# Twenty-eight steps of row preparation ahead of expert 0's last products, where three were

## The chip, the cores and the metric

The kernel runs on one core of a Trainium2 chip. The metric is the device time of one execution in microseconds (us); three runs of the kernel before gave a median of 1004.69 us (1001.67 to 1005.63). One further execution was recorded by the hardware profiler and is the source of every row below.

The core's engines each have a queue that is worked off in order: TensorE (PE in the rows; its weight loads are PEld), VectorE (DVE), ScalarE (ACT), GpSimd (POOL) and SyncE (SP). An instruction whose inputs or buffer are not ready holds up all that stands behind it on its engine.

## The reference

An attention over 32 memory slots gives `x` (4608 rows of 512), and a mixture of 8 experts with the two best per row follows. The change lies in the expert part, of which this is the core:

```python
top2 = np.argpartition(-noisy_logits, 2, axis=1)[:, :2]     # two experts per row
for e in range(E):                                           # 8 experts
    for k in range(2):
        mask = top2[:, k] == e
        h = np.maximum(x[mask] @ w1[e], 0.0)                 # 512 -> 1024
        out[mask] += top2_w[mask, k, None] * (h @ w2[e])     # 1024 -> 512
```

## The kernel before

Attention and routing come first. They write the attention's rows to a table in DRAM (`xs`) and, for each expert, a list of row numbers and weights (`lst`). Each expert then takes up to 1216 rows from its list. All products are made in float16 from a high and a low half of each factor, so that every float32 tile has to be split: ACT copies it to float16 (the high half), and DVE subtracts that copy from it (the low half).

Expert 0 is worked in four groups of rows, called (0,0) to (0,3). The first three are mixed into the attention; the fourth has 448 rows. Every later expert has two groups, of 320 and 288 rows: (1,0), (1,1), (2,0) and so on. For expert 0, `mm1` (line 924) makes the first layer in eight chunks `f` of 12 matmuls (line 935) into one of three PSUM banks `mp`; ACT reads each chunk out (`r`, line 941, two buffers), DVE makes its halves `hh` and `hl` (lines 942 and 943). `mm2` (line 945) makes the second layer (line 965), ACT scales the result by the row weights (`y`, line 977), and POOL adds it to the output with an indirect DMA (line 995).

The later experts use a scheme of seven products for the first layer (`mm1_sums`, line 837; its matmuls are line 851), which takes sums and differences of quarters of the rows and of the weights. The preparation of the rows is `gather_sums` (line 781), a generator that is run in steps. For each of three blocks of a group (128, 128 and 64 pairs of rows for (1,0)) it

- fetches two tiles of rows, `gsum` and `gtile`, by indirect DMAs that POOL issues (line 793);
- makes sums and differences on DVE (lines 810, 811, 825, 826);
- splits three tiles into halves (ACT line 820, DVE line 821), two of 512 columns called `ghalf` and one of 768 called `gsplit`, and has SyncE issue a transposing DMA of each into `xt`, which the matmuls read (line 822). `ghalf` has two buffers in the pool that `gather` uses too, and a third one of its own; a buffer is free again when its transpose has landed.

Between blocks it yields "wait" until a count of ticks has passed (`FAR` and `MOVE`, 8 each). Expert 0's own rows are prepared by `gather` (line 740: fetch in line 757, split in lines 768 and 771, transpose in line 772). The weights of expert 1 are prepared by `w_prep_sums` (line 635): four sums of squares on ACT (line 644), a short chain on DVE that turns them into a scale (lines 647 and 374 to 381, ending in `wsc`), and then splits of the weights and of their sums (ACT line 654, DVE line 657; sums in lines 668 to 672).

The order of the work is made in two stages. The program text calls generators step by step, and each call gets a priority in the order of the calls; a planner then lays out each engine's queue from those priorities and from a model of the time. In the part around the change, `all_rows` (line 1169) chains the row preparation of all groups into one generator `allr`, beginning with (0,3) and then (1,0). `run(it, n)` (line 1003) takes n steps of a generator, and a "wait" that it gets counts as a step and advances the tick by one. `side` holds the generators from which `step_side` (line 1016) takes one step at a time between the products. `pace` (line 775) ties an instruction to a matmul that was issued a little earlier, if there is one on its list; the list is filled only in `step_side`. Ahead of the loop over groups, in order: the weight load of expert 1, the steps of `allr`, and four steps of the weight preparation `pq[1]` (the four sums of squares). The loop begins with (0,3); `need` (line 1176) runs `allr` until the rows of the group at hand are prepared.

Of the kernel before, what the change touches and what calls it, by code (L numbers as in the profile page):

```python
# [61 lines left out]
def tile_attn_moe(ctx, tc, q_t, phi_t, kv, wgn, noise, w1, w2, out):  # L62
# [536 lines left out]
    def w_load(e, i):  # L599
        WS[e, i] = {}  # L600
        loaded[e, i] = ticks[0]
        for c in (3, 0, 1, 2) if e == 1 and i == 0 else (0, 2, 1, 3) if e else range(4):
            s = WS[e, i][c] = mpool.tile([128, 1024], F32, name="stg%d" % c)
            d = nc.sync.dma_start(s, (w1, w2)[i][e, c])
            if e == 0:
                after(d, "kv", BUF["w2" if i else "w1"] + c * BUF["ws"])
# [396 lines left out]
    def run(it, n=10 ** 9):  # L1003
        for _ in range(n):
            x = next(it, "end")
            if x == "end":
                return
            ticks[0] += x == "wait"
# [160 lines left out]
    def all_rows():  # L1169
        for k, x in enumerate(seq):  # L1170
            yield from rows_in(k, *x)
            ready.add(x)
    allr = all_rows()
# [3 lines left out]
            run(it, 1)  # L1177
    pq[1] = prep(1)
    w_load(1, 0)
    run(allr, 3)  # L1180
    run(pq[1], 4)
    side += [allr, pq[1]]
    for k, (e, g) in enumerate(seq):
# [78 lines left out]
```

## Time and profile before

| quantity | value |
|---|---|
| median of three runs | 1004.69 us (1001.67 to 1005.63) |
| profiled execution | 1002.9 us, of which the span from first to last instruction is 1000.9 us |
| TensorE busy | 918.5 us, 92% of the span |
| DVE, ACT, POOL busy | 616.2, 579.4, 337.2 us |
| mean granted TensorE clock | 0.974 of full speed |
| chain that ended last | TensorE 66%, DMA 10%, DVE 9%, ACT 4% |

How to read it: "busy" counts an engine's instructions, not its waits. The chain that ended last follows the program back from its last instruction, at each step to what released that step. The granted clock is 1.00 at 2.4 GHz and 0.50 at 1.2 GHz. In a timeline a bracket gives the idle time of the engine just before an instruction and what released it; a time from one row to another on a different engine is a difference of start times.

### The profile page before, as it was taken

How to read it: one execution, taken by the hardware profiler on the slowest of the kernel's cores; microseconds unless marked ns; L12 is line 12 of the kernel's file. 1: busy time of each engine (PE TensorE's matmuls, PEld its weight loads, DVE VectorE, ACT ScalarE, POOL GpSimd, SP SyncE). 2: the span in 40 equal slices, each digit the busy share in tenths (PEclk: the TensorE clock that was granted, in tenths of full speed). 3: DMA queues.
4: the chain of work that ended last, by engine and by line, in shares of the span. 5: the costliest groups of instructions: out<-in, count | busy, mean ns of one | idle time of the engine just before them, and what ended most of it. 6: DMA issues, size and time to landing. Idle time of an engine off the chain costs nothing.

```text
span 1000.9 us, 17556 instructions
## 1 busy us (share of the span) xinstructions
PE 918.5 (92%) x6440; PEld 540.0 (54%) x6440; DVE 616.2 (62%) x1407; ACT 579.4 (58%) x1187; POOL 337.2 (34%) x307
## 2 busy tenths in 40 slices
PE   3898996989894999999999999999999999999995
PEld 2465654655342555465555656564646564656552
DVE  1547788642662858575866776576849585957140
ACT  3577775532542756656665767576757666765241
POOL 3122654774222142414141514232333323240303
PEclk9999997999997999999999999999999999999997
DMA  9999979937687778776786869586947794775403
GB/s 319 316 308 324 352 268 344 224 83 119 121 140 98 161 120 162 149 146 99 180 151 116 132 147 179 98 163 120 204 85 148 141 213 74 158 123 82 63 1 48
DMA packets 197910, 162.01 MB, mean 162 GB/s; under 512 B 152064, under 2 KB 162496, under 8 KB 195776
## 3 DMA queue, kind: packets, MB, share of 16 engines
q1 hardware_dynamic: 178144, 120.43, 49.2%
q0 software_dynamic: 19680, 40.45, 23.9%
q8 instruction: 51, 0.84, 0.4%
q14 instruction: 35, 0.29, 0.1%
HBM read 86.77 MB, written 41.07 MB: 128 GB/s over the span
## 4 chain that ended last, share of the span: by engine, by line
PE 66%; DMA 10%; DVE 9%; ACT 4%; issue 4%; POOL 2%; SPq 2%; POOLq 0%; ACTq 0%; DVEq 0%
PE ps L965 18%; PE mp L965 15%; PE ps L851 13%; PE mp L851 7%; DMA xt<-ghalf 4%; PE pb L851 3%; PE mp L935 3%; SPq L703 2%; DMA stg<-in_w 1%; PE xp L470 1%; PE xp L355 1%; DMA phs<-in_phi_t 1%; PE tr L435 1%; PE tr L315 1%; DVE wl L657 1%
## 5 line engine op out<-in xcount | busy, mean ns | idle before, releaser
L995 POOL DMA_INDIRECT out<-y,lt x80 | 137.3, 1716 | 269.3 <-ACT y L977 239.1
L965 PEld LDWEIGHTS <-hh 128*128 128x128 f16 (+2 forms) x1504 | 122.3, 99 | 145.2 <-issue 15.9
L851 PE MATMUL ps<-xt,wh 128*128 128x320 f16 (+1 forms) x560 | 140.1, 295 | 17.6 <-DMA xt<-ghalf 15.1
L965 PE MATMUL ps<-wh,hl 128*128 128x512 f16 (+2 forms) x400 | 125.4, 380 | 0.0
L965 PE MATMUL ps<-wl,hh 128*128 128x512 f16 (+2 forms) x400 | 124.9, 380 | 0.0
L965 PE MATMUL ps<-wh,hh 128*128 128x512 f16 (+2 forms) x400 | 121.5, 380 | 0.0
L851 PEld LDWEIGHTS <-wh 128*128 128x128 f16 x896 | 87.0, 98 | 54.7 <-DMA xt<-ghalf 16.1
L965 PE MATMUL mp<-wh,hh 128*128 128x512 f16 (+2 forms) x352 | 113.0, 380 | 3.5 <-ACT hh L864 1.3
L965 PE MATMUL mp<-wl,hh 128*128 128x512 f16 (+2 forms) x352 | 113.0, 380 | 0.0
L965 PE MATMUL mp<-wh,hl 128*128 128x512 f16 (+2 forms) x352 | 112.0, 380 | 0.8 <-DVE hl L865 0.8
L965 PEld LDWEIGHTS <-hl 128*128 128x128 f16 (+2 forms) x752 | 63.1, 99 | 72.5 <-issue 6.9
L851 PE MATMUL ps<-xt,whx 128*128 128x320 f16 (+1 forms) x336 | 96.3, 292 | 0.0
L793 POOL DMA_INDIRECT gtile<-xs,lt x28 | 32.2, 1151 | 186.8 <-DVE ghalf L821 148.6
L654 ACT ACTIVATE wh<-stg,wsc 128x512 f16<-128x512 f32 x112 | 76.1, 713 | 30.8 <-DVE wsc L381 19.6
L570 POOL DMA_INDIRECT lst<-gent,gidx x72 | 72.1, 1002 | 37.0 <-issue 20.0
L657 DVE SCALAR_TENSOR_TENSOR wl<-stg,wsc,wh 128x1024 f16<-128x1024 f32 (+1 forms) x63 | 73.0, 1161 | 14.9 <-ACT wh L654 14.5
L851 PEld LDWEIGHTS <-whx 128*128 128x128 f16 x672 | 65.8, 98 | 28.0 <-issue 3.8
L644 ACT ACTIVATE wl<-stg 128x1024 bf16<-128x1024 f32 x56 | 58.6, 1047 | 28.9 <-DMA stg<-in_w 22.2
L851 PE MATMUL ps<-xt,wl 128*128 128x320 f16 (+1 forms) x280 | 73.7, 295 | 0.0
L857 ACT ACTIVATE r<-ps 128x320 f32<-128x320 f32 (+1 forms) x112 | 46.8, 421 | 39.7 <-PE ps L851 26.4
L793 POOL DMA_INDIRECT gsum<-xs,lt x42 | 48.1, 1144 | 63.1 <-DVE gsplit L821 52.8
L851 PE MATMUL mp<-xt,wh 128*128 128x320 f16 (+1 forms) x224 | 64.8, 292 | 0.9 <-DMA xt<-ghalf 0.7
(214 smaller groups left out, 1852.8 us busy)
## 6 DMA issues: line engine op xcount, KB each, us to landing
stg<-in_w SPq DMA_DIRECT2D x64, 512.0 KB
kvs<-in_kv SPq DMA_DIRECT2D x16, 1024.0 KB
out<-zt SPq DMA_DIRECT2D x38, 256.0 KB
qs<-in_q_t SPq DMA_DIRECT2D x16, 576.0 KB
xs<-xr SPq DMA_DIRECT2D x36, 256.0 KB
phs<-in_phi_t SPq DMA_DIRECT2D x16, 288.0 KB
kvs<-in_kv SPq DMA_DIRECT2D x16, 128.0 KB
xt<-ghalf SPq DMA_TRANSPOSE x88
```

The costliest lines, as they stand in the source:

```text
L315: mark["kv", u] = T.matmul(pk[h * 32:(h + 1) * 32, 0, :], es[:K, c, h * 32:(h + 1) * 32], kvs[:K, c, h, :], start=(c == 0), stop=(c == 4))
L570: sc = G.indirect_dma_start(out=lst[:, :], out_offset=bass.IndirectOffsetOnAxis(ap=idx[:, j, k:k + 1], axis=0), in_=ent[:, j, k, :], in_of ...
L644: (id if first else pace)(A.activation(wl[:, c * 1024:c * 1024 + 1024].bitcast(BF16), s[c], AF.Square, accum_out=am[:, c:c + 1]))
L654: (id if first else pace)(A.activation(h[:, o + k:o + k + 512], x[:, k:k + 512], AF.Identity, scale=sc))
L657: V.scalar_tensor_tensor(l[:, o:o + n], x, sc, h[:, o:o + n], op0=OP.mult, op1=OP.subtract)
L703: d = nc.sync.dma_start(dst, src)
L793: G.indirect_dma_start(out=x[:n], out_offset=None, in_=xs[:, :], in_offset=bass.IndirectOffsetOnAxis(ap=ix.bitcast(I32), axis=0))
L851: mark["pe"] = T.matmul(ps[:, :nh], t[w][:, o:o + 128], xt[:, 4 * k0 + 2 * n0 * lo + 2 * (a - k0) + c, :nh], start=(first and m == 0), sto ...
L857: A.activation(y[:, :nh], ps[:, :nh], AF.Identity, scale=SHC)
L935: d = mark["pe"] = mark["mm1", g] = T.matmul(ps[:, :n], ww[:, c * FF + f * 128:c * FF + (f + 1) * 128], xt[:, xo + c, :n], start=(k == 0), ...
L965: mark["pe"] = T.matmul(ps[lo:lo + x.shape[-1]], x, ws, start=start, stop=stop)
L995: d = G.indirect_dma_start(out=out[:, :], out_offset=bass.IndirectOffsetOnAxis(ap=LT[e][:n, t, 0:1].bitcast(I32), axis=0), in_=y[:n], in_o ...
```

## The change

Line 1180 takes 28 steps of `allr` where it took 3:

```diff
@@ -1177,7 +1177,7 @@
             run(it, 1)
     pq[1] = prep(1)
     w_load(1, 0)
-    run(allr, 3)
+    run(allr, 28)
     run(pq[1], 4)
     side += [allr, pq[1]]
     for k, (e, g) in enumerate(seq):
```

By the generators' text, 8 of the 28 steps prepare (0,3) in full. The rest go into (1,0): the fetch of its first and second block, 8 waits, the sum, the three splits and the differences of its first block, the fetch of the third block, and 4 waits. The ticks stand at 12 when the loop begins, where they stood at 0. No instruction is added to or taken from the program; the planner lays out the queues anew.

DVE at the end of group (0,2), where expert 1's first scale is made (`wam` to `wsa`), as the difference of the two orders; `gsum`, `ghalf`, `gtile` and `gsplit` with lines 810 to 826 are row preparation of (1,0):

```order
 L943 TENSOR_TENSOR hl<-r,hh 128x256
 L771 TENSOR_TENSOR ghalf<-gtile,ghalf 64x512
-L647 TENSOR_REDUCE wam_3596<-wam 128x1
+L647 TENSOR_REDUCE wam_3616<-wam 128x1
+L810 TENSOR_TENSOR gsum<-gtile 128x256
+L821 TENSOR_TENSOR ghalf<-gsum,ghalf 128x512
+L811 TENSOR_TENSOR gtile<-gsum,gtile 128x256
+L821 TENSOR_TENSOR ghalf<-gtile,ghalf 128x512
+L825 TENSOR_TENSOR gsum<-gsum 128x256
+L826 TENSOR_TENSOR gsum<-gsum 128x256
+L821 TENSOR_TENSOR gsplit<-gsum,gsplit 128x768
 L374 TENSOR_REDUCE wsa<-pb 128x1
```

Seven instructions stand between the reduction and the scale now: the sums of the second block (lines 810 and 811) and the splits and differences of the first. The sums of the first block went further up, between the second `CAST hh` of (0,2)'s first layer and the `hl` that belongs to it.

ACT at the same place, before, from the last sum of squares to the read-out of (0,3)'s first chunk (`r`, 448 columns):

```order
L644 ACTIVATE wl_3546,wam<-stg_3534 128x1024
L977 ACTIVATE y<-mp,wlu 128x512
L654 ACTIVATE wh_3545<-stg_3530,wsc 128x512
L654 ACTIVATE wh_3545<-stg_3534,wsc 128x512 x2
L654 ACTIVATE wh_3545<-stg_3532,wsc 128x512
L654 ACTIVATE whx<-stg_3528,wsc 128x512 x2
L941 ACTIVATE r<-mp 128x448
```

and now:

```order
L644 ACTIVATE wl_3591,wam<-stg_3534 128x1024
L820 ACTIVATE ghalf<-gsum 128x512
L820 ACTIVATE ghalf<-gtile 128x512
L977 ACTIVATE y<-mp,wlu 128x512
L820 ACTIVATE gsplit<-gsum 128x768
L654 ACTIVATE wh_3590<-stg_3530,wsc 128x512
L654 ACTIVATE wh_3590<-stg_3534,wsc 128x512 x2
L654 ACTIVATE wh_3590<-stg_3532,wsc 128x512
L654 ACTIVATE whx<-stg_3528,wsc 128x512 x2
L941 ACTIVATE r<-mp 128x448
```

The three copies of the first block came in ahead of the six weight splits, which still stand ahead of the read-out.

ACT at the second layer of (0,3), before, up to the first read-out of (1,0) (`r<-ps`, line 857); the `128x` copies are the second block's, the `64x` ones the third's:

```order
L977 ACTIVATE y<-mp,wlu 128x512
L977 ACTIVATE y<-ps_3820,wlu 128x512
L820 ACTIVATE ghalf<-gtile 128x512
L644 ACTIVATE wl_3810,wam<-stg_3801 128x1024
L820 ACTIVATE gsplit<-gsum 128x768
L644 ACTIVATE wl_3810,wam<-stg_3803 128x1024
L820 ACTIVATE ghalf<-gsum 64x512
L977 ACTIVATE y<-mp,wlu 128x512
L820 ACTIVATE ghalf<-gtile 64x512
L986 ACTIVATE r<-ps_3893 64x512
L820 ACTIVATE gsplit<-gsum 64x768
L857 ACTIVATE r<-ps_3947 128x320
```

and now:

```order
L820 ACTIVATE ghalf<-gsum 64x512
L820 ACTIVATE gsplit<-gsum 64x768
L977 ACTIVATE y<-mp,wlu 128x512
L820 ACTIVATE ghalf<-gtile 64x512
L977 ACTIVATE y<-ps_3842,wlu 128x512
L644 ACTIVATE wl_3820,wam<-stg_3811 128x1024
L644 ACTIVATE wl_3820,wam<-stg_3813 128x1024
L644 ACTIVATE wl_3820,wam<-stg_3815 128x1024
L644 ACTIVATE wl_3820,wam<-stg_3817 128x1024
L977 ACTIVATE y<-mp,wlu 128x512
L986 ACTIVATE r<-ps_3920 64x512
L857 ACTIVATE r<-ps_3954 128x320
```

The second block has left this stretch; of the third, two copies stand ahead of the first `y` and one behind it.

## Rows read from the trace of the kernel before

**Rows 1.** The page's 40 slices of the span: busy tenths of TensorE in each.

```profile
PE   3898996989894999999999999999999999999995
```

**Rows 2.** Waits of TensorE over the span: total us, times, longest us.

```profile
PE ps L851 <- DMA xt<-ghalf: 15.1, 2, 13.7
```

**Rows 3.** Chain of waits around 302 us: start us, us, what.

```profile
301.51 0.69 DVE r L987
...
302.57 11.90 DMA xt<-ghalf
...
314.51 3.38 PE ps L851 x12
```

**Rows 4.** Stretches around 315 us: busy us by engine, then granted clock, DMA share, GB/s.

```profile
310.00:315.00 5.00, 0.49 (x2) 0.28 (x3) 0.00 (x0) 0.00 (x0) 0.00 (x0) 0.50 1.24 144
...
315.00:320.00 5.00, 5.00 (x27) 3.11 (x26) 0.56 (x2) 2.94 (x6) 0.00 (x0) 0.68 0.24 18
```

**Rows 5.** Timeline of ACT, 293 to 296 us: start us, us, instruction, [idle before <- releaser].

```profile
293.59 0.69 ACT L977 ACTIVATE y<-mp,wlu 128x512 f32<-128x512 f32 x1 [7.38 <-PE mp L965]
...
295.25 0.62 ACT L820 ACTIVATE ghalf<-gtile 128x512 f16<-128x512 f32 x1
```

**Rows 6.** Timeline of POOL: gathers of expert 1's first and second block.

```profile
241.16 1.19 POOL L793 DMA_INDIRECT gtile<-xs,lt  x1 [0.30 <-DVE hh L942]
...
254.31 0.98 POOL L793 DMA_INDIRECT gtile<-xs,lt  x1 [10.05 <-DVE wlu L734]
```

**Rows 7.** DMA issues, 236.7 to 237.9 us; then line 793, 225 to 345 us.

```profile
gsum<-xs,lt POOLq DMA_INDIRECT x1, 3.7
...
DMA to landing us min/median/max: 3.7/6.4/9.2
```

**Rows 8.** Timeline of VectorE (DVE), 239 to 286 us.

```profile
239.89 0.48 DVE L943 TENSOR_TENSOR hl<-r,hh 128x256 f16<-128x256 f32 x1
...
257.69 0.29 DVE L374 TENSOR_REDUCE wsa<-pb 128x1 f32<-128x128 f32 x1 [0.42 <-PE pb L372]
...
277.23 0.42 DVE L825 TENSOR_TENSOR gsum<-gsum 128x256 f32<-128x256 f32 x1
...
280.54 1.27 DVE L657 SCALAR_TENSOR_TENSOR wlx<-stg,wsc,whx 128x1024 f16<-128x1024 f32 x1
...
282.04 0.95 DVE L821 TENSOR_TENSOR gsplit<-gsum,gsplit 128x768 f16<-128x768 f32 x1
...
285.38 0.69 DVE L821 TENSOR_TENSOR ghalf<-gsum,ghalf 128x512 f16<-128x512 f32 x1 [0.34 <-ACT ghalf L820]
```

**Rows 9.** Timeline of TensorE (PE), 238 to 284 us.

```profile
238.57 0.60 PE L935 MATMUL mp<-stg,wh 128*128 128x256 f16 x4 [2.42 <-ACT y L977]
...
261.61 0.92 PE L935 MATMUL mp<-xt,wh 128*128 128x448 f16 x4 [3.31 <-DMA xt<-ghalf]
...
267.87 0.92 PE L935 MATMUL mp<-xt,wh 128*128 128x448 f16 x4
...
283.33 0.92 PE L935 MATMUL mp<-xt,wh 128*128 128x448 f16 x4
```

**Rows 10.** Timeline of SyncE's queue (SPq), 249 us.

```profile
249.31 2.65 SPq L772 DMA_TRANSPOSE xt<-ghalf  x2
```

**Rows 11.** Timeline of ACT, 252 to 280 us.

```profile
252.68 0.63 ACT L768 ACTIVATE ghalf<-gtile 128x512 f16<-128x512 f32 x1 [5.27 <-DMA xt<-ghalf]
...
258.76 2.56 ACT L654 ACTIVATE wh<-stg,wsc 128x512 f16<-128x512 f32 x4 [1.11 <-DVE wsc L381]
...
264.13 0.54 ACT L941 ACTIVATE r<-mp 128x448 f32<-128x448 f32 x1 [1.58 <-PE mp L935]
...
279.97 0.83 ACT L820 ACTIVATE gsplit<-gsum 128x768 f16<-128x768 f32 x1
```

**Rows 12.** Stretches of 1 us: busy us by engine, granted clock, DMA share, GB/s.

```profile
241.00:242.00 1.00, 1.00 (x7) 0.69 (x6) 0.47 (x2) 0.00 (x0) 0.84 (x1) 0.50 1.05 180
...
262.00:263.00 1.00, 1.00 (x7) 0.54 (x6) 1.00 (x3) 0.55 (x1) 0.00 (x0) 1.00 0.21 39
```

## The prediction, made before the changed kernel was run

> **What bounds the kernel now.** I read the page's line of slices for TensorE first, then the waits of TensorE, the chain of waits in order of time around the worst of them, the granted clock there, and last the engines' timelines over the 60 us in front of it.
>
> TensorE is the bound. Its line shows nine tenths or more in every slice of 25 us from the fourteenth on, but for the last; the thirteenth (300 to 325 us) has 4 [rows 1]. One wait makes that dip: 13.7 us for a transpose into `xt` [rows 2]. The chain shows what is late. Expert 0's tail tile is finished on DVE at 301.5; a transpose issued at 302.57 needs 11.90 us to land, and only at 314.51 does (1,0) start its products [rows 3]. They then run at half clock at first: the granted clock is 0.50 until 315 and 0.68 on average from 315 to 320 [rows 4]. The reason for the late transposes is on ACT: it stood 7.38 us, until 293.59, for a result `y` of expert 0, and the second block's copy, which does not need `y`, came behind it at 295.25 [rows 5]. So the second and third block are split only after 295 us. DMA service alone is not the cause; the place in ACT's queue is.
>
> **The change, part by part.** Of the 28 steps, the first 9 ran ahead of (0,3) anyway (`need` takes them). New there are 19: 12 waits, two fetches (four gathers on POOL), and the first block's work: two sums and two differences on DVE, three copies on ACT, three low halves on DVE, three transposes on SyncE. Nothing is removed from the program. Since the ticks stand at 12, the second and third block move up too. I cost the places where a queue is now blocked, in order of time.
>
> *First block's sum, on DVE.* It now stands ahead of the `hl` that ran at 239.89 [rows 8], but its gather is issued at 241.16 [rows 6]. Gathers of this line landed 3.7 to 9.2 us after issue, and the one issued just before took 3.7 [rows 7]; so the sum waits until 244.9 to 250.4. Behind it wait (0,2)'s halves, then ACT's two `r` buffers, then TensorE's three banks. The cover is that (0,3) cannot start before its own rows land, at 261.61, with TensorE idle for 3.31 us [rows 9]; those rows hang on SyncE, which issues their transposes from 249.31 [rows 10], and on ACT's copy at 252.68, which waits for a `ghalf` buffer [rows 11]. With 244.9, over seven microseconds remain until 252.68 for the six chunks behind, and the cost is nothing; with 250.4 it is at most the 5.5 us by which that lands later. I take 0, by the nearest gather.
>
> *Scale of expert 1's weights.* It now stands behind the first block's splits, whose second `ghalf` is free only when (0,3)'s last transpose has landed, at about 261.6. From there: ACT copy 0.62 [rows 5], DVE half 0.69, two differences at 0.42, ACT `gsplit` 0.83, DVE `gsplit` 0.95, which gives 265.5 [rows 8, 11]; the scale chain takes 1.07 (257.69 to 258.76), so the splits start at 266.6 instead of 258.76. Second block's gather, issued at 254.31, must land too; with the median 6.4 that is 260.7 and hidden, with 9.2 it is 263.5 and adds at most 2.8. Six splits at 0.64 (2.56 for four) then stand ahead of (0,3)'s first read-out: 270.4, plus 0.54 for itself, 271.0. The third chunk needs that bank and started at 267.87 [rows 9], so TensorE loses 3.1 us. The fourth chunk waits for a bank whose `y` now has two more copies ahead of it on ACT; I put 1.0 on that (estimate; bounds 0 and the two copies, 1.24). The last chunk ends at 288.4 instead of 284.25 (283.33 + 0.92). TensorE then has 16.6 us of second layer (284.25 to 300.9, just before the row at 301.51), so it is done at 305.0. The weights themselves end at 281.8 (280.54 + 1.27) plus 7.8, or 289.6: 15 us of cover.
>
> *Third block.* Its last copy stands behind the first `y`: 293.59 + 4.1 = 297.7, plus 0.69, 0.62 and 0.69, so its transpose is issued at 299.7. Lightly loaded, a transpose landed 3.4 us after issue (249.31 to 252.68); in the jam it took 11.90. That gives 303.1 or 311.6. I take 303.1: the other two blocks and their transposes are gone from the stretch that made the jam. Then rows and weights are there when TensorE comes at 305.0, and (1,0) starts 9.5 us earlier than at 314.51.
>
> *Clock.* The half clock after the stall goes: 0.5 us at half and 5 us at 0.68 give back 0.25 + 1.6 = 1.85 us [rows 4]. The new wait of 3.1 us in (0,3) may bring a new one. After the 2.42 us wait that ended at 238.57 the clock stood at 0.50 at 241; after the 3.31 us wait that ended at 261.61 it was 1.00 at 262 [rows 12]. One says 3 us at half (1.5 lost), the other nothing; I take the middle, 0.8.
>
> The Trainium skill (TensorE: Matmul & The Clock Gate, What's actually happening) calls half clock the default and says that activity releases the throttle; by it the new wait would cost the full 1.5 and the gain would be 9.8. The row at 262 shows an idle stretch of that length without a fall.
>
> *Later stages.* Lists of experts 1 to 3 are reordered as well. The weight splits of expert 1's second layer move up, the (1,1) rows too. The slices there read nine [rows 1], which can hide 2.5 us each; I take 0 between minus 2.5 and plus 2.5.
>
> Sum: 9.5 + 1.85 - 0.8 = 10.5 us less than the profiled execution's 1002.9 (span 1000.9, and 2.0 around it): 992.4. The median of the runs lies 1.8 above that execution, so 994.2.
>
> **The rivals.** *A, the transpose is still last.* If the third block's transpose lands at 311.6, TensorE, after the 12 matmuls that need only an earlier transpose (1.7 us, half of the 3.38 that they took at half clock [rows 3]), stands from 306.7 for 4.9 us and falls to half clock again (1.5, as above). The gain shrinks to 4.1: 1000.6. For it: the DMA share in the jam, 1.24 [rows 4]. Against: the second block's transposes have left that stretch.
>
> The Trainium skill (DMA: Bandwidth & Descriptors, Issuing engines are not separate DMA queues) says that transfers from all engines end on the same 16 DMA engines and interleave; by it an earlier transpose helps only if those 16 are free. The DMA share of 1.24 at 310 to 315 agrees for the old place; no run shows the new one yet.
>
> *B, the gathers land late.* With both at 9.2 us the bounds above, 5.5 and 2.8, come off together: a gain of 2.2 at worst and about 6 in the middle, 998.7. For it: the queue is in order and DVE has nothing else to do meanwhile. Against: the nearest landing, 3.7.
>
> *C, the queues lock step, and it gets slower.* ACT and DVE now alternate between row work, weight splits and TensorE's read-outs in one order, each waiting for the other. Before, the splits from 258.76 to 281.8 took 23 us with the two overlapped. If all overlap went, they would take 23 more; (0,3)'s read-outs stand among them, so its last chunk, and with it the second layer, ends at 328 (305 + 23), 13.5 later than 314.5: 1018.2. It decides from 9.5 us of lost overlap on. For it: the last read-outs stand behind the last sums of the weights. Against: neither engine's waits of 1 to 2 us there are of that size [rows 11].
>
> *D, nothing changes:* as A with a late gather, within 0.5%.
>
> **How the numbers follow.** My forecast 0.60, A 0.14, B 0.13, C 0.08, D 0.05. A measurement of this kernel can tell about 0.5%, 5 us, from no change; so faster means below 999.7. The forecast and B lie below, A mostly above: faster 0.77, same 0.15, slower 0.08. Range: the low end is the forecast without the 4.1 us lost in (0,3) and with 2.5 us found later, 987.6; the high end takes in A and B's worst (1002.5): 987 to 1003.
>
> **What would show it.** In the changed profile: TensorE's wait for `xt` before (1,0) under 3 us instead of 13.7; (1,0) starting near 305 at clock 1.00; a DVE wait of some 5 us near 240 on the gather; a new TensorE wait of about 3 us for ACT's read-out near 268; scale at about 266. I am wrong if (1,0) starts after 311, if (0,2)'s products slip past 261.6, or if more than 5 us of waits appear after 330.

## The result, and the profile after

The changed kernel takes 988.03 us (median of four runs, 986.78 to 989.67); the kernel before took 1005.16 us beside it (four runs, 1001.67 to 1006.39). The ratio is 0.9836 with a 95% interval of 0.9807 to 0.9865, a gain of 17.1 us (13.6 to 19.4 by the interval). The forecast was 994.2, a gain of 10.5, in a range of 987 to 1003. The profiled execution after took 987.7 us with a span of 985.8, which is 15.1 less than the span before.

On the page, TensorE's slices and its granted clock answer to [rows 1]. The 4 in the thirteenth slice is gone; the eleventh (246 to 271 us) has a 7 where it had an 8.

```profile
PE   3999985888799999999999999999999999999994
...
PEclk9999997999999999999999999999999999999998
```

TensorE's longest wait from 255 to 330 us is one of 2.8 us for ACT, and it is new. The 13.7 us of [rows 2] are not there.

```profile
PE mp L935 <- ACT r L941: 2.8, 1, 2.8
```

TensorE's timeline at the start of (0,3), at its third chunk and at the start of (1,0) answers to [rows 3, 9]. (1,0) starts without any wait.

```profile
258.47 0.73 PE L935 MATMUL mp<-xt,wh 128*128 128x448 f16 x3 [2.00 <-DMA xt<-ghalf]
...
267.71 0.92 PE L935 MATMUL mp<-xt,wh 128*128 128x448 f16 x4 [2.81 <-ACT r L941]
...
302.25 0.45 PE L851 MATMUL ps<-xt,wh 128*128 128x320 f16 x2
```

DVE answers to [rows 8]: the first block's sum stands there for its gather, and the scale's chain begins behind the first block's last half.

```profile
241.75 0.42 DVE L810 TENSOR_TENSOR gsum<-gtile 128x256 f32<-128x256 f32 x1 [5.73 <-DMA gtile<-xs,lt]
...
262.37 0.28 DVE L374 TENSOR_REDUCE wsa<-pb 128x1 f32<-128x128 f32 x1
```

ACT answers to [rows 5, 11]: the weight splits wait for the scale; of the third block, two copies come ahead of the first `y` and one right behind it.

```profile
263.45 2.56 ACT L654 ACTIVATE wh<-stg,wsc 128x512 f16<-128x512 f32 x4 [1.98 <-DVE wsc L381]
...
289.49 0.63 ACT L820 ACTIVATE ghalf<-gsum 64x512 f16<-64x512 f32 x1 [2.26 <-PE mp L965]
291.77 0.84 ACT L820 ACTIVATE gsplit<-gsum 64x768 f16<-64x768 f32 x1 [1.65 <-DVE gsum L826]
294.68 0.69 ACT L977 ACTIVATE y<-mp,wlu 128x512 f32<-128x512 f32 x1 [2.06 <-PE mp L965]
295.26 0.62 ACT L820 ACTIVATE ghalf<-gtile 64x512 f16<-64x512 f32 x1
```

The last transpose is issued by SyncE at 296.62, where the one that ended last before was issued at 302.57 [rows 3]:

```profile
296.62 1.19 SPq L822 DMA_TRANSPOSE xt<-ghalf  x1
```

Stretches of TensorE (busy us, granted clock, DMA share, GB/s) answer to [rows 4, 12]. The granted clock falls behind the new wait; at the start of (1,0) it no longer does.

```profile
268.00:269.00 1.00, 1.00 (x6) 0.81 0.00 0
269.00:270.00 1.00, 1.00 (x4) 0.50 0.00 0
...
271.00:272.00 1.00, 1.00 (x4) 0.50 0.23 44
272.00:273.00 1.00, 1.00 (x7) 0.98 1.12 207
...
304.00:306.00 2.00, 2.00 (x17) 1.00 0.72 109
```

Two times cut each execution into three parts: the start of (0,3) and the start of (1,0). They serve for the runs below; each line is one profiled execution. e7 is left out: its first product of (1,0), at 289.27, stands among those of (0,3), so that the cut means something else there.

| kernel | (0,3) starts | (0,3) to (1,0) | (1,0) to the end |
|---|---|---|---|
| before | 261.61 | 52.90 | 686.4 |
| after | 258.47 | 43.78 | 683.6 |
| e4, queues as before | 258.82 | 52.31 | 688.3 |
| e9, queues as after | 312.69 | 43.66 | 681.5 |
| e1 blocks 2 and 3 earlier | 264.75 | 45.99 | 689.5 |
| e2 first block only | 261.31 | 43.20 | 680.5 |
| e3 scale first | 259.46 | 41.03 | 681.4 |
| e5 gathers held | 260.62 | 49.15 | 685.9 |
| e6 scale first, ticks 0 | 259.40 | 45.71 | 684.6 |
| e8 tails whole | 313.62 | 39.35 | 672.5 |

e8 and e9 ran on another chip, where the kernel before takes 1056.08 us; in these two the difference lies ahead of (0,3). Runs are therefore compared by their ratio to the kernel before on the same chip.

### The profile page after: what moved, and what is told of

It reads as the page before. It is cut to its first block, busy times and chain, and to the rows that moved or that the text cites. A ratio compares the mean times of both kernels' runs of the same rounds, so it can differ in the third digit from the quotient of the medians.

```text
span 985.8 us, 17560 instructions
## 1 busy us (share of the span) xinstructions
PE 917.4 (93%) x6440; PEld 537.5 (55%) x6440; DVE 613.3 (62%) x1407; ACT 580.4 (59%) x1187; POOL 336.7 (34%) x307
## 4 chain that ended last, share of the span: by engine, by line
PE 61%; DVE 5%; issue 4%; DMA 4%; SPq 2%; ACT 2%; POOL 2%; POOLq 0%; ACTq 0%
PE ps L965 19%; PE mp L965 16%; PE ps L851 14%; PE mp L851 7%; PE pb L851 4%; DMA xt<-ghalf 3%; SPq L703 2%; PE mp L935 2%; DVE wl L657 1%; POOL lst L570 1%; POOL out L995 1%; DVE wlx L657 1%; DVE yw L861 1%; ACT wh L654 1%; DVE yv L861 1%
## 5 line engine op out<-in xcount | busy, mean ns | idle before, releaser
L793 POOL DMA_INDIRECT gsum<-xs,lt x42 | 45.7, 1087 | 60.3 <-DVE gsplit L821 48.2
L851 PE MATMUL mp<-xt,whx 128*128 128x320 f16 (+1 forms) x224 | 64.9, 293 | 0.0
```

The source lines that it names most:

```text
L793: G.indirect_dma_start(out=x[:n], out_offset=None, in_=xs[:, :], in_offset=bass.IndirectOffsetOnAxis(ap=ix.bitcast(I32), axis=0))
L851: mark["pe"] = T.matmul(ps[:, :nh], t[w][:, o:o + 128], xt[:, 4 * k0 + 2 * n0 * lo + 2 * (a - k0) + c, :nh], start=(first and m == 0), sto ...
```

## The experiments

**e1, e2: what made the transposes late?** The prediction said: the place of the second and third block's copies on ACT, behind the first `y`. e1 moves those blocks alone:

```diff
-            fetched[i] = (n, a, b, ticks[0] + FAR)
+            fetched[i] = (n, a, b, ticks[0] + (4 if (e, g) == (1, 0) else FAR))
-            moved = ticks[0] + MOVE
+            moved = ticks[0] + (4 if (e, g) == (1, 0) else MOVE)
```

> Three steps ahead, as before; but the first group of expert 1 counts 4 ticks instead of 8 between its blocks, so that the second and third block stand earlier in the queues. The first block is not ahead of (0,3): its copies come behind the first read-out of (0,3) on ACT. Theory P (what cost 11.9 us before was the place of the second and third block's copies behind the first y on ACT, and the first block's head start is only a means): (0,3) to (1,0) takes 44 to 47 us (before 52.9, after 43.9) and the time is 988 to 992 us. Rival H (the head start itself counts, since three blocks' transposes cannot land in the 30 us in front of (1,0)): 50 us or more between the two starts, a transpose wait of over 6 us in front of (1,0), and 998 to 1005 us.

e2 has the first block alone ahead:

```diff
     run(allr, 28)
+    ticks[0] = 0
     run(pq[1], 4)
```

> 28 steps ahead, but the ticks are set back to 0 behind them: the first block is ahead of (0,3) as in the changed kernel, while the second block's copies come only behind the sixth read-out of (0,3) on ACT and the third block's last copy behind the third y. Theory P (place of the second and third block): most of the gain is lost, a transpose wait of 3 to 8 us in front of (1,0), 47 to 51 us between the starts of (0,3) and (1,0), time 993 to 1000 us. Rival H (head start of the first block): as the changed kernel, under 45 us, 987 to 990 us.

e1: ratio 0.991 (0.9881 to 0.9938), median 995.45 us, profiled in the slowest of its eight runs (990.1 to 1002.59). The stretch of 46.0 us is inside theory P; the time is not. In this slowest run (0,3) started 3.1 us later and the stages behind (1,0) took 3 us more than in the profiled run before; what the other seven runs lost there is not on record. By the medians e1 brings 8.6 us on its chip, half of what e2 brings. TensorE's start of (1,0), ACT ahead of it, and the landing of the third block's `ghalf` pair in the chain of waits:

```profile
310.74 0.43 PE L851 MATMUL ps<-xt,wh 128*128 128x320 f16 x2 [3.90 <-DMA xt<-ghalf]
```

```profile
293.35 0.63 ACT L820 ACTIVATE ghalf<-gtile 128x512 f16<-128x512 f32 x1 [2.00 <-PE mp L965]
298.77 0.69 ACT L977 ACTIVATE y<-mp,wlu 128x512 f32<-128x512 f32 x1 [4.79 <-PE mp L965]
299.35 0.83 ACT L820 ACTIVATE gsplit<-gsum 128x768 f16<-128x768 f32 x1
```

```profile
304.89 5.80 DMA xt<-ghalf
```

e2: ratio 0.9837 (0.9786 to 0.9887), 987.04 us, the whole gain. Theory P missed by 6 us, and H named the number:

```profile
304.51 0.43 PE L851 MATMUL ps<-xt,wh 128*128 128x320 f16 x2 [0.25 <-DMA xt<-ghalf]
```

```profile
291.17 0.84 ACT L820 ACTIVATE gsplit<-gsum 128x768 f16<-128x768 f32 x1 [0.71 <-PE mp L965]
295.63 0.67 ACT L977 ACTIVATE y<-mp,wlu 128x512 f32<-128x512 f32 x1
...
301.24 0.63 ACT L820 ACTIVATE ghalf<-gtile 64x512 f16<-64x512 f32 x1 [0.32 <-DVE wsb L379]
```

```profile
301.85 2.53 SPq L822 DMA_TRANSPOSE xt<-ghalf  x2
```

What to see here is which copies stand behind the first `y`. Before, two of the second block and all of the third: wait 13.7. In e1, one of the second and all of the third: 3.9. In e2, only the third, and its `ghalf` pair landed within 2.7 us although ACT reached its second copy only at 301.24 (no gather was issued beside it, between 293.3 and 304.7 us). So the third block's place cost 0.25 us ahead of (1,0), and 0.80 behind it for the `gsplit` transpose, against what theory P had said; the second block's place cost more. The first block's head start is one way to get the second ahead of `y`, and e1 shows that another way brings 6.9 of the 9.1 us of the stretch.

The copies' lateness itself was worth little. Counted from the start of (0,3), the third block's `ghalf` pair was issued at 41.0 us before, at 40.1 in e1 and at 40.5 in e2. What changed was the time from issue to landing: 11.9 before, 5.8 in e1, at most 2.7 in e2. In e1 one of the second block's transposes and one gather had moved to 10 us ahead of the pair; in e2 neither the second block's transposes nor gathers were near it.

**e5: what was the jam made of?** The prediction held that DMA service alone was not the cause. In the kernel before, POOL issued four gathers for (1,1) around the third block's `ghalf` transposes, two just ahead of their issue at 302.57 and two while they were on their way:

```profile
298.36 1.29 POOL L793 DMA_INDIRECT gtile<-xs,lt  x1 [0.31 <-issue]
299.95 0.98 POOL L793 DMA_INDIRECT gsum<-xs,lt  x1 [0.30 <-DVE ghalf L821]
...
303.17 1.19 POOL L793 DMA_INDIRECT gtile<-xs,lx  x1 [0.31 <-issue]
...
306.42 0.99 POOL L793 DMA_INDIRECT gsum<-xs,lt  x1 [0.30 <-issue]
```

e5 is the kernel before with those held back:

```diff
+                if (e, g) == (1, 1):
+                    tc.add_manual_dep(d.ins, mark["tail"].ins.name, SYNC, reason="held back")
...
+                if k == 1 and m == 0:
+                    mark["tail"] = mark["pe"]
```

> The kernel before, with one thing added: the gathers of expert 1's second group (four of them were issued between 298 and 307 us, while the third block's transposes were on their way) wait for the first product of (1,0). Transposes, copies and scatters in front of (1,0) keep their order. Theory G (the 11.9 us that the third block's transposes took came from these gathers on the same DMA engines): the transpose lands 3 to 6 us after its issue, the wait in front of (1,0) falls from 13.7 to under 8 us, and 44 to 47 us lie between the starts of (0,3) and (1,0). Rival Q (it came from the second block's transposes, split behind the first y and issued just before): the wait stays at 11 to 14 us and 51 to 54 us lie between the starts. The time may rise in either case, since the rows of (1,1) come later: 998 to 1008 us.

Ratio 0.9904 (0.9871 to 0.9937), 995.99 us. The first gather now follows the first product, and the transposes issued at 304.51 are in at 309.77:

```profile
311.83 1.02 POOL L793 DMA_INDIRECT gsum<-xs,lt  x1 [5.08 <-PE ps L855]
```

```profile
304.51 2.66 SPq L826 DMA_TRANSPOSE xt<-ghalf  x2
```

```profile
309.77 0.45 PE L855 MATMUL ps<-xt,wh 128*128 128x320 f16 x1 [7.11 <-DMA xt<-ghalf]
```

That is 5.3 us from issue to landing instead of 11.9, and a wait of 7.1 instead of 13.7, with ACT's order untouched. Theory G holds for both. Its other two numbers missed: 49.2 us lie between the starts instead of 44 to 47, and the time is 2 us below its range. The stretch is long because (0,3) itself took longer in this execution: the first `y` came 34.8 us behind its start, against 32.0 before. The granted clock stood at 0.50 until 266, which costs 2.9 us; in the kernel before it was 1.00 there [rows 12]:

```profile
262.00:264.00 2.00, 2.00 (x7) 0.50 0.00 0
```

e1 lost 2.9 us to the clock in (0,3) as well (0.50 until 270), so its 46.0 us, too, hold that much that the place of the copies does not explain. The Trainium skill (DMA: Bandwidth & Descriptors, Issuing engines are not separate DMA queues) has transfers from all issuing engines interleave on the same 16 DMA engines; these two landings, 11.9 and 5.3 us, agree with it.

**e3, e6: the price of the scale's place.** e3 makes the first block's copies wait for the scale:

```diff
-    run(allr, 28)
-    run(pq[1], 4)
+    run(allr, 18)
+    run(pq[1], 5)
+    run(allr, 10)
...
+                if (e, g, i) == (1, 0, 0):
+                    tc.add_manual_dep(d.ins, mark["wsc"].ins.name, SYNC, reason="scale first")
```

> 28 steps ahead as in the changed kernel, but the first block's three copies are made to wait for the scale of expert 1's weights, so that the scale stands ahead of them on DVE. Theory S (in the changed kernel the scale's place behind the first block costs TensorE 2.8 us in the third chunk of (0,3) and a fall of the clock to 0.90-0.93 behind it, and both reach the end): the wait near 268 shrinks to under 1 us, (0,3) to (1,0) takes 40.5 to 42.5 us instead of 43.9, time 984 to 986.5 us. Rival G (given back: the third block's transposes come last then): a transpose wait of 2 to 4 us in front of (1,0), time 987 to 989 us.

Ratio 0.9792 (0.9738 to 0.9846), 982.89 us: theory S on the wait and the stretch (41.0 us); the time is 1.1 us below its range. The wait in the third chunk is gone, the splits start 1.8 us behind the start of (0,3) instead of 5.0, and (1,0) still waits for nothing:

```profile
260.24 0.63 ACT L820 ACTIVATE ghalf<-gsum 128x512 f16<-128x512 f32 x1 [3.69 <-DVE wsc L381]
...
261.29 1.32 ACT L654 ACTIVATE wh<-stg,wsc 128x512 f16<-128x512 f32 x2
```

```profile
300.49 0.45 PE L854 MATMUL ps<-xt,wh 128*128 128x320 f16 x2
```

e6 adds `ticks[0] = 0` behind these steps.

> The scale ahead of the first block's copies (as in the third experiment) together with the ticks set back to 0 (as in the second). Theory A (the two add up: 41 us between the starts of (0,3) and (1,0), and the 680.5 us behind it that the second showed): 979 to 982.5 us. Rival L (the third block's last copy stands behind the third y, and with TensorE 2 us earlier at (1,0) its transpose is what ends last): a transpose wait of 2 to 4 us in (1,0), 983 to 986 us.

Ratio 0.9858 (0.9803 to 0.9912), 991.35 us: outside both. The wait that L named is there, and (0,3) lost 2.9 us to the clock where e3 lost 1.7, which together make the stretch 4.7 us longer than e3's. Another 4.1 us were lost behind (1,0) (684.6 us against 680.5 in e2): 1.7 of it is the clock (0.56 and 0.58 from 306 to 310), and no run separates the rest.

```profile
305.11 0.43 PE L854 MATMUL ps<-xt,wh 128*128 128x320 f16 x2 [3.52 <-DMA xt<-ghalf]
```

**e4, e9: what an unchanged order varies by.** e4 takes 9 steps ahead of the squares (`run(allr, 9)`), e9 puts the 28 steps behind them (the two lines exchanged).

> Nine steps ahead of the four squares instead of three, those that ran before (0,3) anyway. The queues are those of the kernel before but for one exchange of two neighbours on ACT. Theory P: no change, 1002 to 1006 us, 52 to 54 us between the starts of (0,3) and (1,0). Rival O (the order against the squares is what pays): 988 to 992 us. It also shows whether the start of (0,3) at 261.6 us before and 258.5 after, ahead of every moved instruction, belongs to the kernel (then 261 to 262 here) or to the execution (then anywhere from 258 to 263).

> The 28 steps stand behind the four squares of expert 1's weights instead of ahead of them. The planner lays out the same queues as in the changed kernel, but for the order of a few weight splits. Theory P (the place of the 28 steps against the squares is worth nothing): as the changed kernel, 986 to 990 us, 43 to 45 us between the starts of (0,3) and (1,0), a wait of 2 to 3.5 us in the third chunk. Rival O (the squares ahead bring the scale forward): 982 to 985 us. It is a second sample of what the start of (0,3) and the stages behind (1,0) take in one and the same order.

e4: ratio 1.002 (0.999 to 1.005). e9: ratio 0.9819 (0.9772 to 0.9866; 1036.72 us on the chip where before takes 1056.08). Theory P both times, for e9 by the ratio. TensorE waits in e4 as before, and in e9 as after (2.81 us both):

```profile
258.82 0.92 PE L935 MATMUL mp<-xt,wh 128*128 128x448 f16 x4 [1.80 <-DMA xt<-ghalf]
...
311.13 0.71 PE L851 MATMUL ps<-xt,wh 128*128 128x320 f16 x2 [13.12 <-DMA xt<-ghalf]
```

```profile
312.69 0.54 PE L935 MATMUL mp<-xt,wh 128*128 128x448 f16 x2 [0.24 <-DMA xt<-ghalf]
...
321.92 0.91 PE L935 MATMUL mp<-xt,wh 128*128 128x448 f16 x2 [2.81 <-ACT r L941]
```

**e7: more steps still** (`run(allr, 51)`).

> 51 steps ahead instead of 28: all three blocks of expert 1's first group are fetched, summed and split ahead of (0,3). One copy of the second block comes into (0,2), the others ahead of (0,3)'s first read-out, and the scale falls behind them. Theory T (the rows are not what (1,0) waits for any more, so more of them ahead only delays the scale and the read-outs of (0,2) and (0,3)): TensorE's waits between 235 and 285 us rise by 3 to 8 us against the changed kernel, 990 to 996 us. Rival M (more head start gains more): 980 to 986 us.

Ratio 0.9819 (0.9789 to 0.9849), 987.36 us. T's waits came, and its time did not; neither theory's range holds the median. TensorE's waits over 0.5 us from 230 to 285 us sum to 16.6 us against 11.2 in the changed kernel. The largest:

```profile
279.44 1.18 PE L965 MATMUL ps<-wh,hh 128*128 128x512 f16 x2 [7.16 <-DVE hh L942]
```

From the start of (1,1) on, e7 took 620.5 us where the changed kernel took 633.9. The weight loads of the second layer (PEld, 366 to 960 us: total idle, times, longest) show one reason, after and then in e7 ("issue" stands where the engine waited for nothing that the profile shows):

```profile
PEld L965 <- issue: 19.2, 49, 0.4
```

```profile
PEld L965 <- issue: 8.3, 21, 0.4
```

In the kernel after these gaps lie where 64-column loads and 128-column loads alternate (128*64 is a load of 64 columns). The products there start 0.30 us apart, and 0.22 where the width stays:

```profile
525.26 0.11 PEld L965 LDWEIGHTS <-hh 128*64 128x64 f16 x2 [0.42 <-issue]
...
525.82 0.33 PEld L965 LDWEIGHTS <-hh 128*128 128x128 f16 x3 [0.41 <-issue]
```

```profile
524.74 0.38 PE L965 MATMUL ps<-wh,hl 128*128 128x512 f16 x1
524.96 0.38 PE L965 MATMUL ps<-wl,hh 128*128 128x512 f16 x1
525.26 0.41 PE L965 MATMUL mp<-wh,hh 128*64 128x512 f16 x2
```

Counted in the traces from the start of (1,1) on, the weights change between narrow and wide 86 times in the kernel after and 48 times in e7. That is not the whole 13.4 us: TensorE's waits there sum to 5.0 us after and to 0.2 in e7.

**e8: tails in one piece, on top of e3.** An order-only dependency ties the first product of each tail tile to the product ahead of it, and the first product of later tiles and groups to the tail's last. By its text the edit holds for all experts behind expert 0, not for 1 to 3 alone.

```diff
+                if e and start:
+                    for o in [was] if i == 4 else [mark["t4"]] if "t4" in mark else []:
+                        tc.add_manual_dep(d.ins, o.ins.name, KEEP, reason="tail in one piece")
```

> The third experiment's kernel (scale ahead of the first block's copies), and the products of every tail tile of experts 1 to 3 (64 or 32 columns of weights at a time) kept in one piece on TensorE, where the order laid out so far puts 128-column products between them. The order has 96 changes between narrow and wide products instead of 134. Theory W (each change costs TensorE 0.1 to 0.2 us, which is why the seventh experiment's stages from (2,0) on took 93.5 us per expert where the changed kernel's took 96): the 681.4 us behind the start of (1,0) shrink to 674 to 678 and the time is 975 to 979.5 us. Rival R (the pieces were a filling, and without them TensorE waits for rows or read-outs at each tail): no gain, 982 to 990 us.

Ratio 0.9712 (0.9662 to 0.9763), the best of all; on the same chip 1026.15 us against 1036.72 for e9, whose queues are those of the changed kernel. Behind the start of (1,0) it takes 672.5 us, 8.9 less than e3 (and than e9, on its own chip), and more than theory W had forecast. By the traces 38 changes of width are gone there (90 in e3, 52 in e8), as W counted; all of the gain would be 0.23 us for each. Not all of it is theirs: from (1,1) on, the distances between the starts of the first layer's 320-column products, whose weights keep their width, sum to 3.2 us less as well (140.2 in e3, 137.0 in e8). That leaves at most 0.15 us for each change. The same gaps in e3 and in e8, in stretches that lie about as far behind (1,0):

```profile
PEld L968 <- issue: 20.0, 51, 0.4
```

```profile
PEld L972 <- issue: 5.9, 14, 0.4
```

The Trainium skill (TensorEngine Tiling (Array Packing), Key Properties) says that changing the tiling mode drains TensorE. The gaps here sit at changes of width and go with most of them; whether such a change is one of mode in the page's sense, no run shows.

## Why the prediction was right, point by point

- **What bounds it, and the dip.** Right in place and size: the wait of 13.7 us went, and the stretch from (0,3) to (1,0) fell by 9.1 us in the first pair of profiles and by 8.7 in the second (e4 and e9). The prediction had 9.5 less 0.8 of clock.
- **Its cause.** Half right. Of the 13.7 us, 1.8 lay ahead of the issue at 302.57 (TensorE stood from 300.79) and 11.9 behind it. The place of the second block's copies in ACT's queue mattered (e1, e2), but through what it put on the DMA engines beside the third block's pair, not through a late issue, which moved by under 1 us. e1 and e2 moved gathers as well, so what the second block's transposes alone cost is not shown. The sentence that set DMA service aside was wrong: e5 leaves ACT's order and takes away 6.6 us of the wait. The term for the third block had it right, in counting on a short landing once the other transposes are gone.
- **First block's sum.** It waited 5.73 us on the gather, as foreseen, and cost 0.6 us in this pair: from the (0,2) product behind `y` to the start of (0,3) it is 23.7 us (234.81 to 258.47), before 23.0 (238.57 to 261.61).
- **Scale chain.** 5.0 us from the start of (0,3) to the first split; the prediction's 266.6 is 5.0 behind 261.61. The third chunk began 9.24 us into (0,3), before 6.26: 3.0 lost, forecast 3.1. The fourth lost nothing, where 1.0 was put.
- **Clock.** Given back at (1,0) as said. The fall in (0,3) was real: 0.81, then 0.50 until 272, some 1.7 us where 0.8 was taken as the middle. This and the fourth chunk cancel: first-layer end 27.3 us into (0,3) by the chain (285.77), forecast 26.8 and 0.8 of clock; second layer 16.5, forecast 16.6. The Trainium skill's rule (TensorE: Matmul & The Clock Gate, What's actually happening), by which the new wait would cost clock, was nearer with 1.5 than the middle. That the fall belongs to the new wait is not shown: before and e4 lost nothing in (0,3), e1, e5 and e6, without that wait, 2.9 us.
- **Third block.** Issued 38.2 us into (0,3), forecast 38.1; it was never waited for, so rival A did not come.
- **Later stages: the step that was mis-sized.** They were put at 0, between minus 2.5 and plus 2.5. Behind the start of (1,0) the order before takes 686.4 and 688.3 us, the order after 683.6 and 681.5: 4.8 less in the mean. The clock at (1,0), which the prediction counted apart, is 1.85 of it in before and 2.8 in e4; some 2.5 is left, at the edge of what was allowed for. Two waits of TensorE before, between the starts of (1,1) and (2,0), are part of that, 2.1 us together. Neither stands in after or e9:

```profile
384.06 0.39 PE L965 MATMUL mp<-wh,hh 128*128 128x512 f16 x1 [1.27 <-ACT hh L864]
...
387.20 0.39 PE L965 MATMUL mp<-wh,hl 128*128 128x512 f16 x1 [0.85 <-DVE hl L865]
```

- **What stays open.** 8.9 and 4.8 make 13.7, inside the measured interval and 3.4 short of its middle. The first pair of profiles differs by 15.1: 9.1, 2.8, and 3.1 by which (0,3) started earlier after. The medians differ by 2.0 more, as the profiled run before was 2.3 us faster than its median and the one after 0.3. That start varies from 258.5 to 261.3 with one block ahead and from 258.8 to 264.8 without, leaving out the chip of e8 and e9; four samples each do not show that the change moves it. What the prediction worked out, the stretch and the clock at (1,0), measured 8.9 and 2.3, or 11.2 us in the mean, against 10.5. What brought the time down to 988.0, 1 us above the low end of the range, it did not have; that this part fell its way is luck.

## What to carry to other kernels

When an engine waits for the last of several transfers, ask both what held up their issue and what else was issued while they were on their way; here the issue moved by less than 1 us in e1 and e2, and the landing fell from 11.9 us to 5.8 when a transpose and a gather beside it were moved away (e1), and to 2.7 at most with neither kind beside it (e2); holding back the gathers alone made it 5.3 (e5). Look at the granted clock before a stretch is compared between runs: 2.9 us of the stretch in e1 and e5 are clock. A block of work that is moved forward pushes what stood there: find the short chain (here five small instructions that make a scale) on which a whole row of later work hangs, and keep it ahead. A planner that lays out all queues anew changes far stages as well, so compare two samples of each stage before a difference there is put to the edit.

## What was not expected of the hardware

- Changing between 64- (or 32-) and 128-column products cost TensorE 0.09 us in the distance of two starts (0.31 instead of 0.22 in the median, from (1,1) on in e3) and at most 0.15 us in all (e8 against e3), with gaps of 0.4 us in the weight loads.
- The third block's pair of transposes landed in 2.7 us (e2), 5.3 us (e5), 5.8 us (e1) and 11.9 us (before), by what else was on the DMA engines.
- A wait of 2.00 us ahead of (0,3) left the clock at 1.00 in the kernel after; the same wait in e3 was followed by 0.50. These rows show the two, after first:

```profile
259.00:260.00 1.00, 1.00 (x8) 1.00 0.21 45
```

```profile
260.00:261.00 1.00, 1.00 (x4) 0.50 0.90 160
```

- One chip took 54 us longer to reach (0,3) (312.7 in e9 against 258.5 us after) and the same from there: 43.66 us to (1,0) in e9, 43.78 after.
